# The last attention head's first three query blocks in the 64x64 form, and the pool of the feed-forward part's transposed rows opened after that head

## The chip, the cores and the metric

The kernel runs on one core of one Trainium2 chip. The metric is the device time of one execution in microseconds (us). Before the change three runs gave 1917.64, 1917.69 and 1917.80 us, so the median is 1917.69 us.

## The reference

`x` has 2048 rows of 640 numbers, there are 32 heads of width 192 with 2048 cached keys and values each, and everything is bfloat16.

```python
xn = layernorm(x)                              # no scale, no shift
q  = (xn @ wq) split into 32 heads of 192
p  = softmax(q @ k_cache^T * 192**-0.5)        # per head, 2048 x 2048
s  = concat_heads(p @ v_cache) @ wo            # 2048 x 640
h  = silu(xn @ w1) * (xn @ w3)                 # 2048 x 1536
g  = silu(h @ w2)                              # 2048 x 640
out = x + s * g
```

## The kernel before

**Tiling.** The 2048 queries are worked in four blocks of 512 (`qb` 0 to 3). In one block of one head the 2048 keys are taken in 8 pairs of 2 x 128 (`p` 0 to 7). For each pair `scores` (L545) makes a 128 x 1024 tile `st` in PSUM, two of which exist; `weights` (L564) sends it through ScalarE's exponential into `pT2` (bf16), and the values are multiplied with `pT2` a pair or two later. At `p == 1` of each block one chunk of other matmuls is slipped in by `extra` (L1006): the query projection of the next head (`project_chunk`, L366), or in the last head (`h` = 31) the first 128 columns of the feed-forward part that no head carries (`hidden_last`, L958, its results `gl`, `ul` and at last `hx`).

**Two forms.** `in_quads` (L157) is true for heads 1 to 30 and false for heads 0 and 31.

- In the 64x64 form (`values_quads`, L627) the values are the stationary operand: twelve matmuls 64x64x512 for a pair, four running at once in the quarters of the array. Scores and projection are cut in 64x64 pieces as well. The output stands transposed (width by query) in two PSUM banks. `evict_quads` (L658) copies one half of a bank with ScalarE (`oa`), adds the other with VectorE (`ot`), and SyncE's queue issues a DMA transpose into `ox`. The sums of the softmax's rows do not come from the matmul: `row_sums` (L672) adds the weight tiles on VectorE (`tree`, then `e`), a second DMA transpose brings `e` to `eT`, and `turned_sums` (L709) reduces `eT` to `rs`, takes reciprocals and writes the scaled rows of `ox` to the staging tile `ostage`: five VectorE instructions. It is put down to run `NPAIR + 3` = 11 steps after `e`.
- In the other form (`values`, L608) the weights are the stationary operand and a column of ones in the value tile gives the row sums; a pair takes sixteen matmuls 64x128x193, two at a time. `evict` (L588) adds the halves on VectorE (`osum`) and scales them into `ostage` directly.

When both heads of a group of two have filled an `ostage` tile, `staged` (L579) stores it to `o_scr` in DRAM.

**Order.** Instructions under `pin` keep the order in which the code is run on their engine. `later` (L669) puts work in a list with a due step, and `do_chores` (L730) runs what is due at the end of each step, one step being one pair. Each engine works through its own list in order, and so does SyncE's DMA queue: a DMA whose data are not ready holds up those behind it.

**Around the last head.** Sixteen groups of 64 columns of the feed-forward part, one for each pair of heads, are made by `swiglu_chunk` (L527) in the odd heads and stored to `hT_scr` when a pair of heads is done; in the last head two chunks each are made in blocks 0 and 1 (`chunks`, L997). At the start of its block 2 the pool of the transposes' and row sums' tiles is closed (`astack.close`) and the pool `hTp` for the feed-forward rows is opened in its room. After the head, `load_hT` reads `hT_scr` back to `hT`, and `ffn_hidden` (L932) makes the rest. Its first call is laid between the last parts of the head's values by `by_halves` (L338): ten matmuls (first half), then a VectorE copy of one column, `mark` (L353), that waits for them, meanwhile eight value matmuls, and then the second ten, whose first one waits for `mark`. The names `w1_sb`, `w2_sb` and `w3_sb` all appear as `w_sb` in the profile. `w2_sb` (1920 KB, L1082) is loaded by POOL's queue into the room of `xnS`, as soon as TensorE has read `xnS` for the last time, which is in `hidden_last` of block 3.

Of the kernel before, what the change touches and what calls it, by code (L numbers as in the profile page):

```python
# [30 lines left out]
def _kernel_impl(ctx, tc, A_x, A_k_cache, A_v_cache, A_wq, A_wo, B_w1, B_w3, B_w2, out):  # L31
    nc = tc.nc
    _, SQ, D = A_x.shape
    _, H, SK, dh = A_k_cache.shape
# [3 lines left out]
    FC = F // P  # L38
    NQT = SQ // P
    NQB = SQ // 512  # L40
    NKT = SK // P
    NPAIR = NKT // 2
# [8 lines left out]
    FCP = FPIG // P  # L51
# [24 lines left out]
    pin = tc.keep_in_program_order  # L76
# [5 lines left out]
    fstack = ExitStack()  # L82
# [73 lines left out]

    def in_quads(h):  # L157
        return 0 < h < H - 1

    def load_ahead(h, qb):  # L160
        if qb == 0:
# [11 lines left out]
    with ExitStack() as actx:  # L173
# [150 lines left out]
        acc = {}  # L324

        def start_head(h):
            L = loads.pop(h)
            heads[h] = dict(
                h=h, L=L, quads=in_quads(h),
                qA=qp.tile([P, SQ], BF16, tag="qA", name="qA"),  # L330
                qF=qfp.tile([P, SQ], BF16, tag="qF", name="qF"),
                qS=qp.tile([P, SQ], BF16, tag="qS", name="qS"),
                qD=qp.tile([DT, SQ], BF16, tag="qD", name="qD"),
                st=stt.tile([P, 5, NQB], F32, tag="st", name="st"),
            )
            pin(nc.vector.memset(heads[h]["st"][:], 0.0))
# [20 lines left out]
        def by_steps(halves, w, qs, quads):  # L357
            for s in range(2 * DC):
                for c in ROWS if quads else (slice(0, P),):
                    for t in range(2):  # L360
                        xs = xnT if s % 2 == t else xnS
                        pin(nc.tensor.matmul(halves[t][c, :], lhsT=w[ROWS[t], s, c], rhs=xs[ROWS[t], s // 2, qs],  # L362
                                             start=(s == 0), stop=(s == 2 * DC - 1)))
# [215 lines left out]
        def staged(h, qb):  # L579
            stages[h // HG, qb][1] -= 1  # L580
            if stages[h // HG, qb][1] == 0:
                g0 = h - h % HG
                keep = pin if in_quads(h) else (lambda x: x)
                acc["store"] = keep(nc.sync.dma_start(
                    out=o_scr[qb].rearrange("(t p) c -> p t c", p=P)[:, :, g0 * DH:(g0 + HG) * DH],
                    in_=stages.pop((h // HG, qb))[0][:, :, :]))
# [82 lines left out]
        def later(wait, f, *a):  # L669
            chores.append((clock[0] + wait, f, a))  # L670
# [4 lines left out]
        def row_sums(hd, qb, p, w):  # L675
            sm = hd["sums"]

            def fours():
                t = aq["tree"].tile([P, 2, 1024], BF16, tag="tree", name="tree")
                a, b = sm["w"]  # L680
                sm["w"] = []
                add(t[:], a[:], b[:])
                sm["t"].append(t)

            def join():
                a, b = sm["t"]
                add(a[:], a[:], b[:])
                sm["t"].pop()

            def fold():  # L690
                t = sm["t"][0]
                add(t[:, 0, :], t[:, 0, :], t[:, 1, :])

            def ends():
                t = sm["t"].pop()[:, 0, :]
                e = aq["two"].tile([P, 512], BF16, tag="e", name="e")
                add(e[:], t[:, 0:512], t[:, 512:1024])
                eT = aq["two"].tile([P, 4, P], BF16, tag="eT", name="eT")
                pin(nc.sync.dma_start_transpose(out=eT[:], in_=e[:]))
# [26 lines left out]
        clock = [0]  # L726
        chores = []
# [12 lines left out]
        heads = {}  # L740
        parts = []
# [11 lines left out]

        def step(hd, qb, p, extra=None):
            me = (hd["h"], qb)
            first = qb == 0 and p < 2
            st2 = scores(hd, qb, p, quads=before["quads"] if first else hd["quads"])
            old = [k for k, _ in parts if k != me]
            old_quads = bool(old) and heads_quads(old[0][0])
            if p == 1 and old_quads:  # L760
                while parts[0][0] != me:
                    next_part()
            pT2 = weights(st2, hd["nb"][qb], p)
            while late:
                late.pop(0)()
            parts.extend((values_quads if hd["quads"] else values)(hd, qb, p, pT2))
            if hd["quads"] and p % 2 == 1:
                row_sums(hd, qb, p, acc["w"])
            if p == 0:
                while sum(k != me for k, _ in parts) > (2 if old_quads else 1):  # L770
                    next_part()
            elif p == 1:
                while parts[0][0] != me:
                    next_part()
            else:
                while len(parts) > (4 + (p > 2) if hd["quads"] else 3):
# [8 lines left out]
        heads_quads = in_quads  # L785
        before = {"quads": False}

        start_head(0)
        L0, m0 = heads[0]["L"], heads[0]["st"][:, 0:3, 0]
# [124 lines left out]
        astack = ExitStack()  # L914
# [40 lines left out]

        last = {}

        def hidden_last(qb, quads):  # L958
            w, g, u = last["w"], last["g"], last["u"]
            qs = slice(qb * 512, (qb + 1) * 512)  # L960
            ps = ps_st.tile([P, 1024], F32, tag="st2", name="ps")
            by_steps((ps[:, 0:512], ps[:, 512:1024]), w, qs, quads)
            pin(nc.vector.tensor_copy(out=g[:, qs], in_=ps[:, 0:512]))
            pin(nc.vector.tensor_copy(out=u[:, qs], in_=ps[:, 512:1024]))

            def gate():
                t = fsb.tile([P, 512], BF16, tag="t", name="t")
                pin(nc.scalar.activation(out=t[:], in_=g[:, qs], func=ACT.Tanh, scale=0.5))

                def product():  # L970
                    a = fsb.tile([P, 512], BF16, tag="a", name="a")
                    pin(nc.vector.scalar_tensor_tensor(out=a[:], in0=t[:], scalar=1.0, in1=g[:, qs], op0=ALU.add, op1=ALU.mult))
                    pin(nc.vector.tensor_tensor(out=hx[:, qs], in0=a[:], in1=u[:, qs], op=ALU.mult))
                return product
            return gate

        for h in range(1, H):
# [16 lines left out]
                todo = [h + 1]  # L994
            else:
                lengths = todo = []
            chunks = [[0], [1], [2], [3]] if h + 1 < H else [[0, 1], [2, 3], [], []]  # L997
            gated = []
            for qb in range(NQB):
                post = []  # L1000
                if (h, qb) == (H - 1, 2):
                    while chores:
                        clock[0] += 1
                        do_chores(h, qb, 2)
                    astack.close()
                    acc["hTp"] = fstack.enter_context(tc.tile_pool(name="hTp", bufs=2, side="right"))  # L1006

                def extra():
                    if h % 2 == 1:
                        for c in chunks[qb]:  # L1010
                            gate = swiglu_chunk(h // 2, heads[h - 1]["qF"], hd["qF"], c)
                            gated.append(gate if hd["quads"] and h > 1 else gate())
                    quads = before["quads"] if qb == 0 else hd["quads"]
                    if h + 1 < H:
                        post.append(project_chunk(h + 1, qb, quads=quads, cast_low=nc.scalar.copy if hd["quads"] else None))
                    else:
                        post.append(hidden_last(qb, quads))

                for p in range(NPAIR):
                    step(hd, qb, p, extra if p == 1 else None)  # L1020
# [14 lines left out]
                        loads[3].update(load_keys(3))  # L1035
                    if (h, qb, p) == (1, 2, 7):
                        copy_keys(3, loads[3])
                    if h + 1 < H:
                        if p == 3 and gated:
                            if hd["quads"] and h > 1:  # L1040
                                later(1, lambda f=gated.pop(0): gated.append(f()))
                            later(3, lambda: gated.pop(0)())
                    else:
                        if p > 4 and gated:
                            gated.pop(0)()
                        if p == 3:
                            gated.append(post.pop()())
# [2 lines left out]
                f(*a)  # L1050
                assert 0, "late"
            heads.pop(h - 1, None)
            before["quads"] = hd["quads"]

        def load_hT(qb):
            for f0, f1 in ((0, FCP // 2), (FCP // 2, FCP)) if qb < NQB - 1 else ((0, FCP),):
# [351 lines left out]
```

## Time and profile before

| | |
|---|---|
| median of 3 runs | 1917.69 us |
| profiled execution | 1917.67 us |
| its span in the trace | 1916.1 us |
| DVE (VectorE) busy | 1438.6 us |
| ACT (ScalarE) busy | 1388.5 us |
| last head, about | 1577 to 1629 us of the span |
| feed-forward rest, about | 1629 to 1705 us |
| output projection | 1705 us to the end |

Times inside the trace count from the start of the span. In a row of a timeline the first number is the start, the second the duration; the bracket at the end tells how long the engine had been idle and what ended that. `PE` is TensorE, `PEld` its weight loads, `SPq` is SyncE's DMA queue, `POOLq` GpSimd's. In a DMA row "to landing" is the time from issue until the data have arrived.

### The profile page before, as it was taken

To read this page: it belongs to the slowest core of one execution; us is meant where nothing else is said; L and a number is where in the kernel's file an instruction comes from. 1 tells how busy PE (TensorE), PEld (TensorE's weight loads), DVE (VectorE), ACT (ScalarE), POOL (GpSimd) and SP (SyncE) were. 2 spreads that over 40 slices of the span, in tenths; PEclk is the share of its full clock that TensorE was granted. 3 is DMA by queue.
4 is the path that set the end of the run, shared out by engine and by line. 5 is a ranking of instruction groups with operands and counts; after the bars stand their busy time and mean duration, and the time that the engine had idled before them with its cause. 6 is when DMAs were issued, how large, how long until landed. Compare 5 with 4: busy or idle time off the path is not lost.

```text
span 1916.1 us, 69138 instructions
## 1 busy us (share of the span) xinstructions
PE 1910.5 (100%) x31063; PEld 1243.5 (65%) x31063; DVE 1438.6 (75%) x2570; ACT 1388.5 (72%) x1533; POOL 141.1 (7%) x223
## 2 busy tenths in 40 slices
PE   9999999999999999999999999999999999999999
PEld 5666666666666666666666666666666666454446
DVE  8688888888888888888888888888888886521111
ACT  7888888888888888888888888888888887210000
POOL 3300000000000000000000000000000000000000
PEclk9999999999999999999999999999999999999999
DMA  7855665656565647565756565656656634936763
GB/s 171 154 98 105 127 120 115 123 114 121 119 127 105 137 101 136 100 136 105 138 99 140 100 129 105 129 105 134 112 115 125 120 69 125 278 76 149 166 151 78
DMA packets 655979, 237.44 MB, mean 124 GB/s; under 512 B 583472, under 2 KB 647568, under 8 KB 655680
## 3 DMA queue, kind: packets, MB, share of 16 engines
q1 hardware_dynamic: 647216, 212.55, 56.1%
q0 software_dynamic: 3776, 15.40, 2.7%
q8 instruction: 243, 3.98, 0.9%
q10 hardware_dynamic: 4688, 5.05, 0.8%
q14 instruction: 56, 0.46, 0.1%
HBM read 54.26 MB, written 31.98 MB: 45 GB/s over the span
## 4 chain that ended last, share of the span: by engine, by line
PE 99%; POOL 0%; DMA 0%; ACT 0%; issue 0%; SPq 0%; DVE 0%; POOLq 0%
PE st L561 34%; PE obank L640 32%; PE ps L362 14%; PE ps_s L1152 8%; PE ps_s L1108 3%; PE obank L620 2%; PE ps_f L1172 2%; PE ps_gu L940 1%; PE ps_f L1188 1%; PE ps L347 0%; DMA KT<-in_A_k_cache_dram 0%; PE ps_gu L347 0%; ACT xnT L290 0%; SPq L115 0%; PE pst L289 0%
## 5 line engine op out<-in xcount | busy, mean ns | idle before, releaser
L569 ACT ACTIVATE pT<-st,nb 128x1024 bf16<-128x1024 f32 x1016 | 1125.4, 1113 | 182.4 <-PE st L561 148.6
L640 PE MATMUL obank<-pT,vt 64*64 64x512 bf16 x11520 | 811.3, 376 | 0.0
L640 PEld LDWEIGHTS <-vt 64*64 64x64 bf16 x11520 | 428.7, 107 | 210.6
L561 PE MATMUL st<-qS,KM 64*64 64x512 bf16 (+1 forms) x1983 | 417.5, 376 | 0.1
L561 PE MATMUL st<-qD,KT 64*64 64x512 bf16 (+1 forms) x1983 | 417.4, 376 | 0.0
L561 PE MATMUL st<-qA,KT 64*64 64x512 bf16 (+1 forms) x1983 | 417.4, 376 | 0.0
L561 PE MATMUL st<-qA,KM 64*64 64x512 bf16 (+1 forms) x1983 | 391.2, 376 | 0.0
L561 PE MATMUL st<-qS,KT 64*64 64x512 bf16 (+1 forms) x1983 | 391.0, 376 | 0.1
L561 PE MATMUL st<-qF,KT 64*64 64x512 bf16 (+1 forms) x1983 | 391.0, 376 | 0.0
L561 PEld LDWEIGHTS <-KT 64*64 64x64 bf16 (+1 forms) x7936 | 289.9, 107 | 138.8 <-issue 0.6
L673 DVE TENSOR_TENSOR tree<-pT,pT 128x2048 bf16<-128x2048 bf16 x240 | 291.8, 1216 | 3.9 <-ACT pT L569 3.4
L362 PE MATMUL ps<-xnT,wq 64*64 64x512 bf16 (+1 forms) x2430 | 292.0, 376 | 0.0
L362 PE MATMUL ps<-xnS,wq 64*64 64x512 bf16 (+1 forms) x2430 | 287.9, 376 | 0.0
L665 DVE TENSOR_TENSOR ot<-oa,obank 128x512 bf16<-128x512 f32 x240 | 154.2, 684 | 147.3 <-ACT oa L664 147.3
L362 PEld LDWEIGHTS <-wq 64*64 64x64 bf16 (+1 forms) x4860 | 176.8, 107 | 89.6
L673 DVE TENSOR_TENSOR tree<-tree 128x2048 bf16<-128x2048 bf16 x240 | 228.9, 954 | 4.1
L561 PEld LDWEIGHTS <-KM 64*64 64x64 bf16 (+1 forms) x3968 | 152.6, 106 | 59.1 <-issue 1.5
L1152 PE MATMUL ps_s<-oT,wo_sb 128*128 128x512 bf16 x720 | 155.7, 379 | 0.0
L664 ACT COPY oa<-obank 128x512 f32<-128x512 f32 x240 | 127.8, 588 | 0.0
L1152 PEld LDWEIGHTS <-wo_sb 128*128 128x128 bf16 x720 | 70.4, 98 | 84.9 <-issue 0.2
L385 ACT CAST qF<-ps 128x512 bf16<-128x512 f32 x127 | 74.5, 586 | 59.3 <-PE ps L362 59.3
L1142 DVE SCALAR_TENSOR_TENSOR tmp<-ps_s,gT 128x512 f32<-128x512 f32 x15 | 10.3, 687 | 136.0 <-PE ps_s L1152 136.0
(159 smaller groups left out, 1427.8 us busy)
## 6 DMA issues: line engine op xcount, KB each, us to landing
o_scr<-ostage SPq DMA_DIRECT2D x64, 384.0 KB, 4.4
vt<-in_A_v_cache_dram SPq DMA_DIRECT2D x62, 384.0 KB, 5.1
qS<-qA SPq DMA_DIRECT2D x240, 64.0 KB, 2.0
qD<-qF SPq DMA_DIRECT2D x120, 64.0 KB, 2.1
KM<-KT SPq DMA_DIRECT2D x60, 128.0 KB, 5.0
wo_sb<-in_A_wo_dram POOLq DMA_DIRECT2D x1, 7680.0 KB, 30.1
wq<-in_A_wq_dram SPq DMA_DIRECT2D x29, 160.0 KB, 3.7
hT_scr<-hblk SPq DMA_DIRECT2D x16, 256.0 KB, 3.2
```

What stands on the lines that cost most here:

```text
L362: pin(nc.tensor.matmul(halves[t][c, :], lhsT=w[ROWS[t], s, c], rhs=xs[ROWS[t], s // 2, qs], start=(s == 0), stop=(s == 2 * DC - 1)))
L385: pin(c(out=dst[:, qs], in_=src))
L561: pin(nc.tensor.matmul(st2[c, t * 512:(t + 1) * 512], lhsT=k[:, c], rhs=q[ROWS[t], qs], start=(s == 0), stop=(s == 2)))
L569: pin(nc.scalar.activation(out=pT2, in_=st2[:], func=ACT.Exp, scale=SCALE, bias=nb[:]))
L620: pin(nc.tensor.matmul(acc["o"][b][:, r, (j % 2) * 256:(j % 2) * 256 + DH + 1], lhsT=pT2[ROWS[r], t * 512 + j * P:t * 512 + (j + 1) * P], ...
L640: pin(nc.tensor.matmul(acc["o"][low][ROWS[c], r, :], lhsT=vt[ROWS[r], u, p, c0:c0 + DT], rhs=pT2[ROWS[r], u * 512:(u + 1) * 512], start=(p ...
L664: pin(nc.scalar.copy(out=oa[:], in_=bank[:, 0, :]))
L665: pin(nc.vector.tensor_tensor(out=ot[:, k * 512:(k + 1) * 512], in0=oa[:], in1=bank[:, 1, :], op=ALU.add))
L673: pin(nc.vector.tensor_tensor(out=out, in0=a, in1=b, op=ALU.add))
L1108: pin(nc.tensor.matmul(ps, lhsT=oT[:, k, :], rhs=wo_sb[:, k, c0:c1], start=(k == 0), stop=(k == OC - 1)))
L1152: pin(nc.tensor.matmul(ps_of[d], lhsT=wo_sb[:, k, d * P:(d + 1) * P], rhs=part(k // KQ)[:, k % KQ, :], start=(k == 0), stop=(k == OC - 1)))
L1172: pin(nc.tensor.matmul(ps[:, e * 512:(e + 1) * 512], lhsT=w2_sb[:, fc, d * P:(d + 1) * P], rhs=rhs[fc], start=(fc == 0), stop=(fc == FC - 1)))
```

## The change

The form is now asked for by block: `block_quads(h, qb)` is true for heads 1 to 30 and also for blocks 0, 1 and 2 of head 31. Block 3 of head 31 stays in the other form.

```diff
+    def block_quads(h, qb):
+        return in_quads(h - 1) if qb < 0 else in_quads(h) or (h == H - 1 and qb < NQB - 1)
...
-                later(NPAIR + 3, turned_sums, hd, qb, eT)
+                later(NPAIR + 3 if block_quads(hd["h"], qb + 1) else 4, turned_sums, hd, qb, eT)
...
         def step(hd, qb, p, extra=None):
             me = (hd["h"], qb)
-            first = qb == 0 and p < 2
-            st2 = scores(hd, qb, p, quads=before["quads"] if first else hd["quads"])
+            quads = block_quads(*me)
+            st2 = scores(hd, qb, p, quads=block_quads(hd["h"], qb - 1) if p < 2 else quads)
...
-            parts.extend((values_quads if hd["quads"] else values)(hd, qb, p, pT2))
-            if hd["quads"] and p % 2 == 1:
+            parts.extend((values_quads if quads else values)(hd, qb, p, pT2))
+            if quads and p % 2 == 1:
                 row_sums(hd, qb, p, acc["w"])
...
-        def hidden_last(qb, quads):
+        def hidden_last(qb, quads, now):
...
             by_steps((ps[:, 0:512], ps[:, 512:1024]), w, qs, quads)
+            if now:
+                pin(nc.scalar.copy(out=u[:, qs], in_=ps[:, 512:1024]))
             pin(nc.vector.tensor_copy(out=g[:, qs], in_=ps[:, 0:512]))
-            pin(nc.vector.tensor_copy(out=u[:, qs], in_=ps[:, 512:1024]))
+            if not now:
+                pin(nc.vector.tensor_copy(out=u[:, qs], in_=ps[:, 512:1024]))
...
-            chunks = [[0], [1], [2], [3]] if h + 1 < H else [[0, 1], [2, 3], [], []]
...
-                if (h, qb) == (H - 1, 2):
-                    while chores:
-                        clock[0] += 1
-                        do_chores(h, qb, 2)
-                    astack.close()
-                    acc["hTp"] = fstack.enter_context(tc.tile_pool(name="hTp", bufs=2, side="right"))
+                now = block_quads(h, qb)
...
-                    if h + 1 < H:
+                    if h + 1 < H or now:
                         if p == 3 and gated:
-                            if hd["quads"] and h > 1:
+                            if now and h > 1:
                                 later(1, lambda f=gated.pop(0): gated.append(f()))
                             later(3, lambda: gated.pop(0)())
+                        if p == 3 and h + 1 == H:
+                            later(3, lambda f=post.pop(): post.append(f()))
+                            later(4, lambda f=post: f.pop()())
...
-        assert FC - FCP == NQB
+        assert FC - FCP == NQB and not chores
+        astack.close()
+        acc["hTp"] = fstack.enter_context(tc.tile_pool(name="hTp", bufs=2, side="right"))
         load_hT(0)
```

In the last head one `swiglu_chunk` is now made in each of the four blocks, so the store to `hT_scr` follows block 3's. The row sums of block 2 are used 4 steps after their `e` and not 11.

On VectorE, at the end of the last head's block 3 before the change: `gl` and `ul` of block 3, then the scaling of block 2's second half, the gate's product (`a`, `hx`), and `mark`.

```order
L963 CAST gl_36485<-ps_38507 128x512
L964 CAST ul_36486<-ps_38507 128x512
L598 RECIPROCAL rl_all_73<-osum_38504 128x2
L599 TENSOR_TENSOR ostage_37897<-osum_38504,rl_all_73 128x2x192
L972 SCALAR_TENSOR_TENSOR a_38643<-t_38592,gl_36485 128x512
L973 TENSOR_TENSOR hx_1518<-a_38643,ul_36486 128x512
L353 COPY mark_38709<-eps_t_68 128x1
```

And there after the change, from the product of the last `swiglu_chunk` (`pa`, `hblk`) on. Ahead of these rows stand now, behind `gl` and `ul`, the end of block 2's row sums (two `tree` additions and `e`) and the five instructions of block 1's `turned_sums`. `eT_38694` and `ox_38602` belong to block 2.

```order
L543 SCALAR_TENSOR_TENSOR pa_38778<-pt_38610,qF_35281 64x512
L545 TENSOR_TENSOR hblk_37730<-pa_38778,qF_36488 64x512
L716 TENSOR_REDUCE rs_38807<-eT_38694 128x4
L718 RECIPROCAL rl_all_73<-rs_38807 128x4
L721 TENSOR_TENSOR ostage_37899<-ox_38602,rl_all_73 128x4x128
L724 TENSOR_TENSOR ox_38602<-ox_38602 128x4x64
L725 TENSOR_TENSOR ostage_37899<-ox_38602,rl_all_73 128x4x64
L975 SCALAR_TENSOR_TENSOR a_38814<-t_38720,gl_36485 128x512
L976 TENSOR_TENSOR hx_1518<-a_38814,ul_36486 128x512
L356 COPY mark_38862<-eps_t_68 128x1
```

Between `gl` and `mark` there now stand the row sums and both `turned_sums`, and the reduction that reads `eT_38694` and the scaling that reads `ox_38602` wait for DMA transposes of block 2.

On SyncE's DMA queue before the change, from the last head's last transpose on:

```order
L699 DMA_TRANSPOSE eT_37817<-e_37815 128x4x128
L584 DMA o_scr0_60<-ostage_37309 128x4x384
L1057 DMA hT_38695<-hT_scr_64 128x4x512
L1057 DMA hT_38735<-hT_scr_64 128x4x512
L544 DMA hT_scr_64<-hblk_37730 64x2048
```

And after the change, where six more transposes are in the queue, the last two of them here:

```order
L587 DMA o_scr0_60<-ostage_37309 128x4x384
L669 DMA_TRANSPOSE ox_38602<-ot_38601 128x8x128
L702 DMA_TRANSPOSE eT_38694<-e_38692 128x4x128
L587 DMA o_scr1_61<-ostage_37613 128x4x384
L547 DMA hT_scr_64<-hblk_37730 64x2048
L587 DMA o_scr2_62<-ostage_37899 128x4x384
L1055 DMA hT_38848<-hT_scr_64 128x4x512 x2
```

The store to `hT_scr` and all four loads of `hT` now stand behind block 2's transposes and behind the store of block 2's `ostage`.

More of the change, by code (lines that the diff above doesn't have):

```diff
@@ L755, in step @@
             me = (hd["h"], qb)
[L756 to L757 removed]
+            quads = block_quads(*me)
+            st2 = scores(hd, qb, p, quads=block_quads(hd["h"], qb - 1) if p < 2 else quads)
             old = [k for k, _ in parts if k != me]
[L759 removed]
+            old_quads = bool(old) and block_quads(*old[0])
             if p == 1 and old_quads:
@@ L1000, in _kernel_impl @@
                 post = []
[L1001 to L1006 removed]
+                now = block_quads(h, qb)
                 def extra():
                     if h % 2 == 1:
[L1010 to L1013, printed above, removed]
+                        gate = swiglu_chunk(h // 2, heads[h - 1]["qF"], hd["qF"], qb)
+                        gated.append(gate if now and h > 1 else gate())
+                    quads = block_quads(h, qb - 1)
                     if h + 1 < H:
[L1015 removed]
+                        post.append(project_chunk(h + 1, qb, quads=quads, cast_low=nc.scalar.copy if now else None))
                     else:
[L1017 removed]
+                        post.append(hidden_last(qb, quads, now))
                 for p in range(NPAIR):
```

9 lines of the change are left out of this document (3 added, 6 removed).

## The prediction

> **What bounds the kernel now.** I read the page first, then the chain of waits, then the timelines of the last head. The page's first group and the chain's shares by engine:
>
> ```profile
> PE 1910.5 (100%) x31063; PEld 1243.5 (65%) x31063; DVE 1438.6 (75%) x2570; ACT 1388.5 (72%) x1533; POOL 141.1 (7%) x223
> PE 99%; POOL 0%; DMA 0%; ACT 0%; issue 0%; SPq 0%; DVE 0%; POOLq 0%
> ```
>
> TensorE is never without work, and the chain that ends last is TensorE for 99% of the span. So a TensorE instruction saved is time saved, whatever another engine does extra is free, and a wait forced on TensorE is paid in full. Both signs must be looked for there. The chain's pieces "in order of time" give the length of a block, since the projection stands at `p == 1` of each: the gaps below are one block of head 30, then blocks 0, 1 and 2 of head 31.
>
> ```profile
> 1565.12 2.16 PE ps L362 x40
> ...
> 1577.64 2.16 PE ps L362 x40
> ...
> 1590.46 2.16 PE ps L362 x20
> ...
> 1603.14 2.16 PE ps L362 x20
> ...
> 1615.81 2.16 PE ps L362 x20
> ```
>
> Differences: 12.52 us in the 64x64 form, 12.82 where the form changes, then 12.68 and 12.67 in the other form.
>
> **Term 1, the form.** Blocks 0 to 2 took 12.82 + 12.68 + 12.67 = 38.17 us and will take 3 x 12.52 = 37.56. The change of form moves into block 3 and costs there 12.82 - 12.675 = 0.145 more than now. Sum: -0.61 + 0.145 = **-0.46 us**. That is all there is to gain: no other TensorE work goes.
>
> ScalarE and VectorE have to follow in the shorter blocks. VectorE gets `tree`, `e`, `ot` and `turned_sums` for `osum`, as in head 30, where this fits. ScalarE gets `oa`, `ul` and a second gate activation (`t`) a block. In head 29, which has one gate activation (`pt`) a block, the exponentials catch up:
>
> ```profile
> 1522.30 2.11 ACT L569 ACTIVATE pT<-st,nb 128x1024 bf16<-128x1024 f32 x2
> 1524.59 1.11 ACT L569 ACTIVATE pT<-st,nb 128x1024 bf16<-128x1024 f32 x1 [0.18 <-PE st L561]
> ```
>
> Two back to back take 2.11, so one costs 1.00 there against 1.29 of TensorE's time for a pair, and 0.18 us are idle. `t` now stands in that place and takes 0.52; the next exponential comes 0.34 late and the one after it is on time. `pt` delays one by about as much (0.29) and head 29's blocks are no longer for it, so I take nothing; if a delay of 0.34 showed in each of three blocks, it would be 1.0 us.
>
> **Term 2, the wait at the end of the head.** After block 3 the first feed-forward tile is made in two halves, and its second half waits for VectorE's `mark`:
>
> ```profile
> 1626.02 1.24 PE L347 MATMUL ps_gu<-xnT,w_sb 64*128 64x512 bf16 x10
> 1627.10 0.50 PE L620 MATMUL obank<-vt,pT 64*128 64x193 bf16 x8
> 1627.52 1.25 PE L347 MATMUL ps_gu<-xnT,w_sb 64*128 64x512 bf16 x10
> 1627.31 0.15 DVE L353 COPY mark<-eps_t 128x1 f32<-128x1 f32 x1 [4.18 <-PE ps_gu L347]
> ```
>
> Now VectorE is idle 4.18 us before `mark`, which ends at 1627.46; TensorE goes on 0.06 later. After the change the first half ends 0.46 earlier and the second could start at 1627.06. But by the order VectorE has, between block 3's `gl` and `mark`, the row sums of block 2, both `turned_sums`, and two products. I time them from block 0 of head 31, where block and form change as they now will in block 3, three blocks of 12.52 = 37.56 earlier:
>
> ```profile
> 1580.08 0.68 DVE L963 CAST gl<-ps 128x512 bf16<-128x512 f32 x1
> ...
> 1583.25 0.42 DVE L673 TENSOR_TENSOR e<-tree 128x512 bf16<-128x512 bf16 x1
> 1583.60 0.68 DVE L713 TENSOR_REDUCE rs<-eT 128x4 f32<-128x512 bf16 x1
> ...
> 1585.79 0.68 DVE L540 SCALAR_TENSOR_TENSOR pa<-pt,qF 64x512 bf16<-64x512 bf16 x1
> 1586.50 0.42 DVE L542 TENSOR_TENSOR hblk<-pa,qF 64x512 bf16<-64x512 bf16 x1
> ...
> 1587.90 0.68 DVE L972 SCALAR_TENSOR_TENSOR a<-t,gl 128x512 bf16<-128x512 bf16 x1
> 1588.61 0.42 DVE L973 TENSOR_TENSOR hx<-a,ul 128x512 bf16<-128x512 bf16 x1
> ```
>
> Shifted: `e` of block 2 ends at 1621.23; block 1's `turned_sums` (1583.60 to 1585.79 = 2.19) ends at 1623.35; `hblk` is done at 1624.4. From there block 2's `turned_sums` 2.19, `a` and `hx` 1.05, `mark` and 0.06: 3.46 us from the moment T at which its `rs` can start until TensorE's second half starts. If `eT` is there, T = 1624.41 and the half starts at 1627.87: 0.35 later than now. So **even undisturbed the wait (0.81) eats the 0.46**.
>
> T depends on when `eT` of block 2 lands. Its issue is at 1621.27, its `ox` goes out at 1617.75. Undisturbed, in block 0 of head 31 (views of SyncE's queue, and of the DMA issues and packets of 1580 to 1584 and of 1583.5 to 1587.5):
>
> ```profile
> 1580.19 1.23 SPq L666 DMA_TRANSPOSE ox<-ot  x1
> q1 hardware_dynamic: 1056, 0.26, 35.4%
> 1583.71 1.19 SPq L699 DMA_TRANSPOSE eT<-e  x1
> q1 hardware_dynamic: 544, 0.13, 31.5%
> ox<-ot SPq DMA_TRANSPOSE x1, 3.1
> eT<-e SPq DMA_TRANSPOSE x1, 3.2
> ```
>
> 1056 and 544 packets, 3.1 and 3.2 us; by the slices of the first view the 1056 move in 1.4 us and end 2.55 after issue, so 0.55 passes until the landing. 3.2 us for `eT` (block 2's would land at 1624.5). But POOL loads `w2_sb` just then, because it waits for the last read of `xnS`, in block 3's projection. Its issue, a store of SyncE's queue issued in the midst of it, their landings, and the packets of the two queues (q0 is POOL's) in 1620.5 to 1624 (one row) and in 1624 to 1626 (two):
>
> ```profile
> 1618.27 1.06 POOL L1082 DMA_DIRECT2D w_sb<-in_B_w_dram  x1 [53.39 <-PE ps L362]
> 1620.02 0.38 SPq L584 DMA_DIRECT2D o_scr<-ostage  x1
> w_sb<-in_B_w_dram POOLq DMA_DIRECT2D x1, 1920.0 KB, 8.9
> o_scr<-ostage SPq DMA_DIRECT2D x1, 384.0 KB, 7.9
> q0 software_dynamic: 217, 1.11, 89.7%
> q0 software_dynamic: 138, 0.70, 87.8%
> q1 hardware_dynamic: 122, 0.09, 13.9%
> ```
>
> In the first stretch SyncE's queue moved no packet at all, in the second 122 beside the load's 138, and the store landed at 1627.9, 0.7 after the load. So I expect the two transposes to be held until the load is through. The load moved data from about 1620.0 to 1626.4; the projection now ends 0.62 earlier (37.56 + 1579.80 against 1617.98), so to 1625.8. `ox` has some 0.45 us before it starts, 340 of its packets; during the load about 120 pass, as of that store; of 1600 some 1140 are left, at 1056 in 1.4 us another 1.5 us: 1627.3. With 0.6 from the last packet to the landing T = 1627.9, the second half starts at 1627.9 + 3.46 = 1631.36, a wait of 4.30. Everything behind follows TensorE and shifts alike.
>
> The bounds: T = 1624.4 (wait 0.81) and, if nothing passes beside the load and the landing tail is 1.4, T = 1629.1 (wait 5.5). Between stands the nearest case with a smaller load, 2 x 160 KB of `wl` at 1517.52:
>
> ```profile
> wl<-in_B_w_dram POOLq DMA_DIRECT2D x2, 160.0 KB, 4.1
> ox<-ot SPq DMA_TRANSPOSE x1, 5.5
> eT<-e SPq DMA_TRANSPOSE x1, 4.4
> ```
>
> There `ox` took 2.4 more than its usual 3.1 though the load was a sixth. I take the row with `w2_sb`, since it is the same load at the same place.
>
> [...]
>
> **Terms at nothing.** The loads of `hT` move behind `hblk`'s store and block 2's `o_scr` store:
>
> ```profile
> 1640.21 3.62 PE L1172 MATMUL ps_f<-hT,w_sb 128*128 128x512 bf16 x16
> hT<-hT_scr SPq DMA_DIRECT2D x2, 512.0 KB, 4.0
> ```
>
> `ostage` of block 2 is ready at T + 2.2 = 1630.1, the `hblk` store lands by about 1631, so the first `hT` lands at about 1636, and its reader is now at 1644: 8 us of cover. If that were gone, TensorE would wait for what is over. The other DMAs of the tail are released by TensorE's and VectorE's tail and shift with it. The pool opened later changes no instruction of TensorE.
>
> **Sum.** 1917.67 (this execution; the median is 1917.69) - 0.46 + 4.30 = **1921.5 us**.
>
> **Rivals.**
> (a) The transposes pass beside the load as if it were not there: T = 1624.4, 1917.67 - 0.46 + 0.81 = 1918.0, not slower in any way one could measure. For it: transposes move small packets in a queue of their own. Against it: the store that moved nothing. It decides if `eT` lands before about 1624.5.
> (b) They are held partly, as beside `wl`: `eT` 4.4 to 4.9 us, T = 1625.7 to 1626.2, 1919.3 to 1919.8.
> (c) Only the saving shows: `mark` isn't late, because T comes early and VectorE is ahead of block 0's pace: 1917.2. VectorE would have to gain 0.8 us; nothing shows that.
> (d) The wait also cools TensorE. At the start of the kernel, after 1.9 us of idleness, the same matmul is half as fast:
>
> ```profile
> 1.88 5.54 PE L224 MATMUL fill<-ones_w,ones_bf 128*128 128x512 bf16 x13 [1.88 <-DVE cols L189]
> 7.53 0.81 PE L224 MATMUL fill<-ones_w,ones_bf 128*128 128x512 bf16 x3
> ```
>
> 0.43 us each against 0.22 us later, though the profile's clock row stands at full there. If a gap of 4.3 us does the same, 3.4 to 5.5 us at half speed lose 1.7 to 2.8: 1923.2 to 1924.3. Against it: no gap in the trace lasts so long, so nothing shows when the speed falls. [...]
> (e) The change doesn't save on TensorE, since ScalarE's extra activation stalls it: +1.0 on the forecast, 1922.5.
>
> **Chances.** Forecast (held until the load is through, 1920.3 to 1922.8) 0.60, (a) 0.07, (b) 0.12, (c) 0.03, (d) 0.14, (e) 0.04. The range from 1918.0 to 1924.0 holds (a) to most of (d); the forecast's own range is 1920.3 to 1922.8. What can be told from no change is 0.2%, 3.84 us, so the line is at 1921.5, on the forecast itself: I give 0.37 of its 0.60 to the upper side (the bound above is as far as that below, but a landing tail is more easily longer than shorter), with (d) and (e) 0.55 slower, 0.43 within, and 0.02 faster, for which no row has the time.
>
> **What would show it.** Right: the projection chunks of head 31's blocks 0 to 2 12.52 apart; VectorE idle before the last `rs` until a DMA; `eT` of block 2 landing with or after `w2_sb`; `mark` starting near 1631; TensorE without work for about 4 us before the second half. Wrong: `eT` landing in 2.4 to 3.2 us; the second half at 1627.9 or earlier; a gap before `ps_f` that ends with a DMA of `hT`; blocks longer than 12.52 with idle TensorE at `st`; feed-forward matmuls at half pace behind the gap.

## The result and the profile after

| | before | after |
|---|---|---|
| time, median of the runs beside each other | 1917.73 us (6 runs, 1917.55 to 1917.84) | 1925.75 us (6 runs, 1924.92 to 1926.29) |
| ratio, 95% interval | | 1.0041 [1.003, 1.0052] |
| profiled execution, its span | 1917.67, 1916.1 | 1924.92, 1923.4 |
| mean granted clock | 1.0 | 0.998 or 0.999 in all six runs |

The change makes the kernel slower by 0.4%: 8.0 us in the medians, 7.25 in the two profiled executions, which the readings below account for. All times are us.

The chain of waits after, the pieces of the last two heads' projections and what follows them:

```profile
1564.94 2.16 PE ps L365 x40
...
1577.46 2.16 PE ps L365 x40
...
1589.98 2.16 PE ps L365 x40
...
1602.50 2.16 PE ps L365 x40
```

The gaps, one block of head 30 and then blocks 0 and 1 of head 31, are now all 12.52; before they were 12.52, 12.82 and 12.68. Block 2 takes 12.52 as well, by the first matmuls of its projection and of block 3's (1602.30 and 1614.82). The shorter form is there, and TensorE's rows from 1577 to 1625 show no stall beside it.

TensorE's timeline behind block 3, to be held against the rows of before in the prediction:

```profile
1625.38 1.24 PE L350 MATMUL ps_gu<-xnT,w_sb 64*128 64x512 bf16 x10
1626.46 0.50 PE L623 MATMUL obank<-vt,pT 64*128 64x193 bf16 x8
1632.18 2.32 PE L350 MATMUL ps_gu<-xnT,w_sb 64*128 64x512 bf16 x10 [5.23 <-DVE mark L356]
1634.29 1.50 PE L623 MATMUL obank<-vt,pT 64*128 64x193 bf16 x16
1635.73 11.26 PE L940 MATMUL ps_gu<-xnT,w_sb 128*128 128x512 bf16 x49
1646.83 3.62 PE L1172 MATMUL ps_f<-hT,w_sb 128*128 128x512 bf16 x15
```

Two things are to be seen. TensorE stands still for 5.23 before the second half of `ps_gu`. And that second half, ten matmuls that took 1.25 before, takes 2.32.

VectorE's timeline says what `mark` was behind:

```profile
1623.88 0.42 DVE L545 TENSOR_TENSOR hblk<-pa,qF 64x512 bf16<-64x512 bf16 x1
1628.71 0.69 DVE L716 TENSOR_REDUCE rs<-eT 128x4 f32<-128x512 bf16 x1 [4.42 <-DMA eT<-e]
...
1631.64 0.42 DVE L976 TENSOR_TENSOR hx<-a,ul 128x512 bf16<-128x512 bf16 x1
1631.98 0.15 DVE L356 COPY mark<-eps_t 128x1 f32<-128x1 f32 x1
```

VectorE itself idles 4.42, until the transpose `eT` of block 2 lands. From there to TensorE's second half pass 1632.18 - 1628.71 = 3.47.

The DMA issues of 1617 to 1630, with their size and the time to landing, then the packets of 1617 to 1620.5, of 1619 to 1621 and of 1621 to 1625 (q0 is POOL's queue with the load of `w_sb`, q1 is SyncE's with the transposes):

```profile
w_sb<-in_B_w_dram POOLq DMA_DIRECT2D x1, 1920.0 KB, 10.8
ox<-ot SPq DMA_TRANSPOSE x1, 7.9
eT<-e SPq DMA_TRANSPOSE x1, 7.6
```

```profile
q1 hardware_dynamic: 777, 0.20, 45.1%
```

```profile
q1 hardware_dynamic: 870, 0.22, 82.5%
q0 software_dynamic: 25, 0.13, 16.9%
```

```profile
q0 software_dynamic: 279, 1.43, 102.2%
q1 hardware_dynamic: 32, 0.00, 0.5%
```

Up to 1620.5 no packet of the load has passed. `ox` has 1056 packets, and 1024 of them are through by 1621. Then the load has the engines nearly to itself. The 32 packets of SyncE's queue in these 4 us are the last of `ox`, which lands at 1625.5; `eT` stands behind them. The first packet of the load comes at 1620.7, 3.2 behind its issue at 1617.48. In the ten profiles here in which no `ox` is under way at that time it comes 1.7 to 1.8 behind its issue (before: 1618.27 and 1620.00), in the four in which one is, 3.2 to 4.1 (after, e3, e4, e6).

The granted clock, in windows of 0.5 us (window, length, busy time of PE, PEld, DVE, ACT and POOL, then PEclk, DMA share and GB/s):

```profile
1629.00:1629.50 0.50, 0.00 (x0) 0.00 (x0) 0.47 (x2) 0.00 (x0) 0.00 (x0) 1.00 1.22 465
1629.50:1630.00 0.50, 0.00 (x0) 0.00 (x0) 0.47 (x2) 0.00 (x0) 0.00 (x0) 0.53 0.33 131
1632.50:1633.00 0.50, 0.50 (x4) 0.15 (x2) 0.00 (x0) 0.00 (x0) 0.00 (x0) 0.50 1.04 306
1636.00:1636.50 0.50, 0.37 (x2) 0.18 (x2) 0.50 (x2) 0.00 (x0) 0.12 (x1) 0.64 1.06 326
1636.50:1637.00 0.50, 0.50 (x3) 0.26 (x3) 0.47 (x2) 0.00 (x0) 0.50 (x2) 1.00 0.85 283
```

A window at 0.53 was at half clock for 94% of it, one at 0.64 for 72%. So the clock is halved from 1629.53 to 1636.36: it falls 2.6 after the last matmul ended and is back 4.2 after TensorE resumed.

The end of the program: VectorE's last instruction, and the last store, before and then after:

```profile
1913.26 0.29 DVE L1115 TENSOR_TENSOR res<-tmp,xt 128x128 bf16<-128x128 f32 x1
```

```profile
out_dram<-res ACTq DMA_DIRECT2D x1, 32.0 KB, 1.4
```

```profile
1919.88 0.29 DVE L1115 TENSOR_TENSOR res<-tmp,xt 128x128 bf16<-128x128 f32 x1
```

```profile
out_dram<-res ACTq DMA_DIRECT2D x1, 32.0 KB, 2.0
```

The account, before to after, in the profiled executions:

| piece | working | us |
|---|---|---|
| start of the kernel (not of the change: it differs from run to run) | projection in head 30's block 1 at 1539.91 against 1540.09 | -0.18 |
| shorter form | first half of `ps_gu` at 1625.38 against 1626.02, less the line above | -0.46 |
| wait for `mark` | first to second half 6.80 against 1.50 | +5.30 |
| half clock | second half to `ps_f` 14.65 against 12.69 | +1.96 |
| from `ps_f` to VectorE's last start | 273.05 against 273.05 | 0.00 |
| end | the rest of 7.25 | +0.63 |

### The profile page after: what moved, and what is told of

Read it like the earlier page. It is cut to its first block, busy times and chain, and to the rows that moved or that the text cites. A ratio compares the mean times of both kernels' runs of the same rounds, so it can differ in the third digit from the quotient of the medians.

```text
span 1923.4 us, 69363 instructions
## 1 busy us (share of the span) xinstructions
PE 1910.1 (99%) x31148; PEld 1243.6 (65%) x31171; DVE 1449.6 (75%) x2579; ACT 1392.4 (72%) x1542; POOL 141.1 (7%) x223
## 4 chain that ended last, share of the span: by engine, by line
PE 98%; DMA 1%; DVE 0%; issue 0%; ACT 0%; POOL 0%; SPq 0%; POOLq 0%
PE st L564 34%; PE obank L643 33%; PE ps L365 14%; PE ps_s L1152 8%; PE ps_s L1108 3%; PE ps_f L1172 2%; PE ps_gu L940 1%; PE obank L623 1%; PE ps_f L1188 1%; DMA eT<-e 0%; PE ps L350 0%; DMA KT<-in_A_k_cache_dram 0%; PE ps_gu L350 0%; DVE tree L676 0%; ACT pT L572 0%
## 5 line engine op out<-in xcount | busy, mean ns | idle before, releaser
L643 PE MATMUL obank<-pT,vt 64*64 64x512 bf16 x11808 | 831.6, 376 | 0.0
L643 PEld LDWEIGHTS <-vt 64*64 64x64 bf16 x11808 | 439.8, 107 | 216.1
L676 DVE TENSOR_TENSOR tree<-pT,pT 128x2048 bf16<-128x2048 bf16 x246 | 299.1, 1216 | 3.9 <-ACT pT L572 3.4
L668 DVE TENSOR_TENSOR ot<-oa,obank 128x512 bf16<-128x512 f32 x246 | 158.1, 684 | 151.3 <-ACT oa L667 151.3
L676 DVE TENSOR_TENSOR tree<-tree 128x2048 bf16<-128x2048 bf16 x246 | 234.6, 954 | 4.2
```

The lines of the kernel that those rows point to most:

```text
L643: pin(nc.tensor.matmul(acc["o"][low][ROWS[c], r, :], lhsT=vt[ROWS[r], u, p, c0:c0 + DT], rhs=pT2[ROWS[r], u * 512:(u + 1) * 512], start=(p ...
L668: pin(nc.vector.tensor_tensor(out=ot[:, k * 512:(k + 1) * 512], in0=oa[:], in1=bank[:, 1, :], op=ALU.add))
L676: pin(nc.vector.tensor_tensor(out=out, in0=a, in1=b, op=ALU.add))
```

## The experiments

Each ran beside the kernel before, whose median there was 1917.77 to 1917.83.

**e1, two blocks instead of three.** Blocks 0 and 1 of head 31 take the 64x64 form, block 2 doesn't, so that the `eT` of block 2 is not late.

```diff
-        return in_quads(h - 1) if qb < 0 else in_quads(h) or (h == H - 1 and qb < NQB - 1)
+        return in_quads(h - 1) if qb < 0 else in_quads(h) or (h == H - 1 and qb < NQB - 2)
```

> The 64x64 form in blocks 0 and 1 of the last head only; block 2 goes back to the other form, so its two transposes are gone, and the last pair of transposes is block 1's, issued about 12.5 us before w2_sb is loaded. Theory (TensorE loses by waiting for mark behind block 2's transposes, which the load of w2_sb holds up, and by the slow clock after it): no wait before the second half, clock full throughout, and two blocks' saving, 2 x 0.155 = 0.3 us: 1917.4 us. Rival 1 (the cost lies in the later opening of the pool and the later hT loads): still about 8 us slower than before. Rival 2 (the form itself saves nothing): 1917.7.

Measured: 1918.74 (1918.42 to 1919.05, 11 runs), ratio 1.0005 [0.9996, 1.0014]. TensorE does not wait for `mark` and the clock is 1.0 (0.999 in one run of eleven): wait and half clock both belong to the third block. But the two shorter blocks do not give their 0.30 + 0.16 - 0.145 = 0.31 either: the first half of `ps_gu` starts at 1626.11 in the chain against 1626.19, and 0.03 of that is the start. The chain leaves TensorE in block 2 and comes back to it in block 3:

```profile
1603.88 1.29 DVE ot L668 x2
...
1618.71 0.61 DVE ul L967
1619.36 0.82 PE st L564 x6
```

For 15 us it runs over VectorE, which has the row sums of two blocks one behind the other there, and the six `st` at its end take 0.82, where the next six take 0.65. That this is where the rest of the 0.31 went is read from the chain alone; no run tried it. The remaining 0.8 to before arises after VectorE's last row (see g1 and g2).

**e2, the code of the change with the form of before.** `block_quads` gives `in_quads(h)`, so that only the later opening of the pool and the code paths remain.

```diff
-        return in_quads(h - 1) if qb < 0 else in_quads(h) or (h == H - 1 and qb < NQB - 1)
+        return in_quads(h - 1) if qb < 0 else in_quads(h)
```

> Everything of the change but the form: blocks 0 to 2 in the form of before, one feed-forward chunk in each block of the last head, the pool opened behind the head, the store of hblk and the hT loads late. Theory: no term in the time, 1917.7 us within 0.3. Rival (late hT loads or the pool stall the feed-forward part): a gap at ps_f and up to 8 us more.

Measured: 1917.81 (1917.67 to 1918.41, 11 runs), ratio 1.0 [0.9991, 1.0009]; first half of `ps_gu` at 1626.03 against 1626.02. This part costs nothing.

**e3, an attempt to hold the load.** The load of `w2_sb` written to be issued after block 2's `rs`.

```diff
-    nc.gpsimd.dma_start(out=w2_sb[:], in_=B_w2.rearrange("(c p) d -> p c d", p=P))
+    with tc.issue_after(acc["rs"].ins):
+        nc.gpsimd.dma_start(out=w2_sb[:], in_=B_w2.rearrange("(c p) d -> p c d", p=P))
```

> As after, but POOL issues the load of w2_sb only when VectorE has read block 2's eT. Theory: ox and eT land in 3.1 to 3.2 us, T is 1624.4 in the frame of before, the wait shrinks from 5.2 to about 0.8 us and the clock stays full: 1918.0 us, and w2_sb lands at about 1634, before its first reader. Rival (the transposes are slow for a reason of their own, not for the load): eT still takes over 7 us and the time stays at 1925 or more.

Measured: 1925.58 (1924.97 to 1927.4, 5 runs), ratio 1.0042 [1.0028, 1.0055]. The edit set an order among instructions but no wait: the load went out at 1617.89, right behind the last projection, as without it. So nothing was held, and this is the changed kernel once more. It shows how far the two transfers vary: in its profile `eT` took 9.1 to land, `w_sb` 12.4, and TensorE waited 6.76.

**e4, `mark` by ScalarE.** The same ineffective hold, and `mark` copied by ScalarE, so that TensorE's second half no longer stands behind VectorE's row.

```diff
-                          nc.vector.tensor_copy, between)
+                          nc.scalar.copy, between)
```

> As the run with the load held, and mark is made by ScalarE, idle at that place, instead of VectorE. Theory: the remaining 0.8 us of wait goes too and only the form's saving is left: 1917.2 us, less than before. Rival (VectorE's late work is paid in the next wait, for the tiles ps_gu that it empties): 1917.5 to 1918.

Measured: 1923.3 (1922.22 to 1924.68, 8 runs), ratio 1.0027 [1.0017, 1.0038]. The second half starts at 1627.08 without a wait, and TensorE waits a little later instead, for a `ps_gu` tile that VectorE has to empty. Its VectorE and TensorE rows:

```profile
1630.21 0.69 DVE L716 TENSOR_REDUCE rs<-eT 128x4 f32<-128x512 bf16 x1 [5.74 <-DMA eT<-e]
```

```profile
1634.80 5.52 PE L940 MATMUL ps_gu<-xnT,w_sb 128*128 128x512 bf16 x17 [3.54 <-DVE a L947]
```

So `mark` is only where the lateness of VectorE is met first. Its cause is ahead of VectorE.

**f5, the load really held.** A data wait of the load on block 2's `rs`, so that the transposes have the DMA engines without it.

```diff
-    nc.gpsimd.dma_start(out=w2_sb[:], in_=B_w2.rearrange("(c p) d -> p c d", p=P))
+    load = nc.gpsimd.dma_start(out=w2_sb[:], in_=B_w2.rearrange("(c p) d -> p c d", p=P))
+    tc.add_manual_dep(load.ins, acc["rs"].ins.name, mybir.DependencyInfo(
+        mybir.DependencyClass.Sync, mybir.DependencyReason.DATA), reason="hold")
```

> The changed kernel, with the 1920 KB load of w_sb made to wait for the reduction rs of block 2, so that the transposes of ot and e of block 2 no longer share the DMA engines with it. Theory (the load holds the transposes up): eT lands in 2.5 to 3.3 us instead of 7.6, ox in about 3.1 instead of 7.9, rs starts near 1624.4 instead of 1628.7, TensorE's wait for mark falls from 5.23 to about 0.8, the granted clock stays at 1.0 throughout, and the time is 1917.9 to 1918.8. Rival (the transposes are late for a reason of their own, such as their queue or the store of hT): eT still takes over 6 us, the wait stays over 4 and the time at or above 1924. Third outcome: the load, now late, collides with the loads of hT, and TensorE waits ahead of the output blocks; then the wait for mark is gone and the time is still above 1919.5.

Measured: 1919.11 (1918.8 to 1921.78, 11 runs), ratio 1.0008 [0.9999, 1.0017]. The load is issued at 1625.88. The DMA issues of 1617 to 1640, VectorE and TensorE:

```profile
ox<-ot SPq DMA_TRANSPOSE x1, 3.9
eT<-e SPq DMA_TRANSPOSE x1, 2.4
```

```profile
1624.30 0.42 DVE L545 TENSOR_TENSOR hblk<-pa,qF 64x512 bf16<-64x512 bf16 x1
1624.64 0.67 DVE L716 TENSOR_REDUCE rs<-eT 128x4 f32<-128x512 bf16 x1
```

```profile
1628.10 1.25 PE L350 MATMUL ps_gu<-xnT,w_sb 64*128 64x512 bf16 x10 [0.72 <-DVE mark L356]
```

`eT` lands in 2.4 and not 7.6, `rs` follows `hblk` without a gap, the wait falls to 0.72 and the second half takes 1.25 again. The load now runs beside SyncE's stores and loads, which pass with it. The packets of 1631 to 1632:

```profile
q0 software_dynamic: 62, 0.32, 86.5%
q1 hardware_dynamic: 61, 0.05, 13.9%
```

That `eT` is on time as soon as the load is issued later shows the load as the cause of the late transposes. One run of the eleven, 1921.78, has a mean clock of 0.999; its gap is not known. No wait for `hT` appears. The time is 0.3 above what was expected, since the end of the program costs 1.0 here (last store 2.3).

**f6, the load held and `mark` by ScalarE.** Both edits above.

> As the run before, and mark is written by ScalarE instead of VectorE, so that TensorE's second half of the first ps_gu no longer stands behind rs, a and hx of block 2. Theory (the wait for mark is the transposes plus VectorE's row): no wait there at all, and some 0.8 less than the run before: 1917.2 to 1918.0. Rival (VectorE's lateness is only passed on to the next place that needs it, the ps_gu tile that VectorE empties): a wait of 0.5 to 1 us in the first ps_gu groups of L940 instead, and the same time as the run before.

Measured: 1918.38 (1918.07 to 1918.6, 11 runs), ratio 1.0003 [0.9994, 1.0012]: 0.73 less than f5. TensorE has no wait between 1617 and 1700. With the transposes in time, VectorE's own row behind `mark` was the last 0.72, and the tiles of L940 are emptied early enough. Yet it is not faster than before, since the end still costs 0.6.

**e6, TensorE kept busy in the gap.** The changed kernel, with 18 matmuls that nobody reads ahead of the wait.

```diff
+        def keep_warm():
+            parts.pop(0)[1]()
+            for _ in range(18):
+                pin(nc.tensor.matmul(warmer[:, 0:512], lhsT=ones_bf[:], rhs=xnT[:, 0, 0:512], start=True, stop=True))
...
-        rest = ffn_hidden(0, 1, ps_st.tile([P, 1024], F32, tag="st2", name="ps_gu"), parts.pop(0)[1])
+        rest = ffn_hidden(0, 1, ps_st.tile([P, 1024], F32, tag="st2", name="ps_gu"), keep_warm)
```

> The changed kernel, with 18 matmuls of 512 columns into a tile that nobody reads put between the two halves of the first ps_gu, ahead of the wait for mark (4 to 5 us of TensorE work at full clock). Theory (about 2 of the 8 us are a clock that halves because TensorE stood still for 5.2 us): mark comes no earlier, the second half starts at the same time (near 1632) but the granted clock stays at 1.0, and the time is 1.7 to 2.0 below the changed kernel's: 1923.5 to 1924.2. Rival (the half clock is not due to the standing still, or it delays nothing because the waits behind it take it up): 1925.4 to 1926.

Measured: 1923.73 (1923.06 to 1925.66, 6 runs), ratio 1.0032 [1.002, 1.0045], 2.0 below the changed kernel. TensorE's timeline:

```profile
1627.16 4.06 PE L1078 MATMUL warmer<-xnT,ones_bf 128*128 128x512 bf16 x17
1633.15 1.25 PE L350 MATMUL ps_gu<-xnT,w_sb 64*128 64x512 bf16 x10 [1.93 <-DVE mark L356]
1634.24 0.83 PE L623 MATMUL obank<-vt,pT 64*128 64x193 bf16 x16
1635.00 11.00 PE L940 MATMUL ps_gu<-xnT,w_sb 128*128 128x512 bf16 x49
1645.84 3.62 PE L1179 MATMUL ps_f<-hT,w_sb 128*128 128x512 bf16 x15
```

Here `mark` comes even 1.0 later (1633.15 against 1632.18), and still `ps_f` starts 1.0 earlier: from the second half to `ps_f` it takes 12.69, as before the change, and not 14.65. The half clock is a consequence of TensorE's standing still, and it costs 1.96. (In the medians part of the 2.0 is the end: this kernel's last store lands in 1.4.)

**e7 and e8, the wait alone.** The kernel before, with 11 and with 14 operations on VectorE ahead of `mark`; no transfer and no form is changed.

```diff
+        for _ in range(11):
+            junk = fsb.tile([P, 512], BF16, tag="u", name="junk")
+            pin(nc.vector.scalar_tensor_tensor(out=junk[:], in0=xnT[:, 0, 0:512], scalar=1.0, in1=xnT[:, 1, 0:512], op0=ALU.add, op1=ALU.mult))
```

> The kernel before, with 11 extra VectorE operations of 512 elements per partition queued ahead of mark, so that TensorE waits for mark as in the change, but for VectorE's work alone and with no transfer moved: a wait of about 2.5 us. Theory (a standing TensorE costs its wait, and keeps its clock if the gap stays below the 2.6 us after which it halved in the changed kernel): time above before by the wait as the waits show it, 1920.0 to 1920.6, clock 1.0 throughout. Rival (each such gap costs more than itself): over 1921.5.

> The run before with 14 instead of 11 extra VectorE operations: a wait of about 4.5 us at the same place. Theory (past some 2.6 us of standing still the clock halves for some 7 us, as in the changed kernel): a half clock in the trace between about 1629.5 and 1636.5, and the time above before by the wait plus 1.7 to 2.0: 1924.0 to 1924.4. Rival (the half clock needs the changed kernel's transfers or its other form): clock 1.0 throughout and the wait alone, 1922.1 to 1922.5.

Measured: e7 1920.92 (1919.82 to 1922.06, 10 runs), ratio 1.0015 [1.0006, 1.0025]; e8 1923.63 (1923.18 to 1923.69, 7 runs), ratio 1.003 [1.0019, 1.0041]. The median of e7 describes no run: its runs fall in two groups of five, 1919.82 to 1920.29 with a mean clock of 1.0 and 1921.55 to 1922.06 with 0.999. The profiled one is of the second group; the gaps of the others are not known. TensorE's waiting row and the clock of e7:

```profile
1630.11 1.83 PE L347 MATMUL ps_gu<-xnT,w_sb 64*128 64x512 bf16 x10 [2.27 <-DVE mark L353]
```

```profile
1630.00:1630.50 0.50, 0.39 (x4) 0.21 (x6) 0.05 (x1) 0.00 (x0) 0.00 (x0) 1.00 0.00 0
1630.50:1631.00 0.50, 0.50 (x7) 0.22 (x4) 0.00 (x0) 0.00 (x0) 0.00 (x0) 0.65 0.00 0
...
1634.00:1634.50 0.50, 0.50 (x4) 0.26 (x3) 0.47 (x2) 0.00 (x0) 0.50 (x2) 0.94 0.00 0
```

A gap of 2.27 costs 2.3 in half of the runs (1917.83 + 2.27 = 1920.1) and some 1.5 more in the other half. In the profiled one of these the clock falls at 1630.65, when TensorE is already working again, and is back at 1634.06: 3.4 later. In e8 the gap is 4.07, all seven runs have the half clock, it lasts from 1631.21 to 1634.62, again 3.4, and 1917.83 + 4.07 + 3.4 / 2 = 1923.6, as measured. The rival for e8, that the changed kernel's transfers or form are needed, falls; so does my bound of 2.6 in e7, under which a gap would keep its clock. In the changed kernel the half clock lasts 6.8, twice 3.4.

**f9, g1 and g2, the last 0.6.** f9 is the kernel before with 11 small copies more on ScalarE. g1 is f6 with the 13 filler matmuls at TensorE's start cut into 31 of 215 columns, 36 instructions more. g2 is the kernel before with them cut into 121 of 56 columns, 216 instructions more, which is as many as the change adds.

```diff
-        keep_busy(13)
+        keep_busy(31, 215)
```

> The kernel before, with 11 copies of one element per partition by ScalarE added in the output stage, where ScalarE has time to spare (some 0.2 us each). Theory (the 0.6 to 0.8 us at the very end of the changed kernel is one more fetch of instructions, 16 KB, for ScalarE's longer program, which lands between the last stores): TensorE's part ends within 0.1 of before, the last store takes 2.0 instead of 1.4, and the time is 1918.3 to 1918.6. Rival (the end belongs to the change itself, or to another engine's program): 1917.6 to 1917.9.

> The run with the load held and mark on ScalarE, and the 13 filler matmuls of 512 columns with which TensorE begins replaced by 31 of 215 columns (the same columns, 36 more instructions of TensorE). Theory (the 0.6 at the very end is a fetch of TensorE's instructions, 16 KB at a time, that falls between the last two stores; 36 more instructions bring it forward by 18 times 52.32 / 384 = 2.5 us): the fetch lies near 2 us ahead of VectorE's last instruction, the last store takes 1.4 again, 2.8 to 3.0 us from VectorE's last start to the end of the span instead of 3.46, and 1917.6 to 1917.9, some 0.6 below that run and level with before. Rival (the end has nothing to do with the length of TensorE's program): 1918.2 to 1918.6.

> The kernel before, with the 13 filler matmuls of 512 columns at TensorE's start replaced by 121 of 56 columns, so that TensorE's program is exactly as long as the changed kernel's (216 instructions more) and nothing else differs. The start may come some us later or earlier by this, and is left out of the reading. Theory (as in the run before): from VectorE's last start to the end of the span it takes 3.4 to 3.6 us as in the changed kernel, instead of 2.84, and the last store 2.0 instead of 1.4, with a fetch packet between the last two stores. Rival: 2.8 to 2.9, and 1.4.

Measured: f9 1917.79 (11 runs), ratio 1.0 [0.9991, 1.0009]: 11 more instructions of ScalarE do nothing. g1 1917.63 (1917.42 to 1917.85, 11 runs), ratio 0.9999 [0.999, 1.0008]: 0.75 below f6. g2 1919.18 (1918.73 to 1920.21, 11 runs), ratio 1.0007 [0.9998, 1.0016]; 0.69 of it is a later start (1540.78 against 1540.09). VectorE's last row and the last store of g1, then of g2:

```profile
1913.11 0.29 DVE L1117 TENSOR_TENSOR res<-tmp,xt 128x128 bf16<-128x128 f32 x1
```

```profile
out_dram<-res ACTq DMA_DIRECT2D x1, 32.0 KB, 1.4
```

```profile
1913.96 0.29 DVE L1115 TENSOR_TENSOR res<-tmp,xt 128x128 bf16<-128x128 f32 x1
```

```profile
out_dram<-res ACTq DMA_DIRECT2D x1, 32.0 KB, 2.2
```

g2's span ends at 1917.6, 3.64 behind its row, where before it is 2.84. The queue that the page lists as `instruction` (q8) moves one packet near the end in each of the fourteen kernels. In before, e2, e6 to e8, f9 and g1 it moves some 1.5 to 1.8 ahead of the start of VectorE's last row and the last store takes 1.4 or 1.5; in after, e1, e3, e4, f5, f6 and g2 it moves 0.2 to 0.3 behind that start, about when the last store goes out, and that store takes 2.0 to 2.4. The kernel before gets the late packet when nothing but the filler matmuls of TensorE's start is cut into more instructions, f6 loses it in the same way. So the place depends on TensorE's program. That the packet carries TensorE's own instructions, and that it is what holds the store, is argued from the two always going together; no row names the engine. Why it falls in one of two places stays open: e1, with 144 instructions more than before, has it where 216 more have it, so it does not simply move with their number.

## Why the prediction was wrong

Forecast 1921.5 with 1918.0 to 1924.0; it was 1925.75. The direction was right, slower by over 0.2%, and so was the mechanism of the wait; the half clock behind the wait and the end were left out of the sum. That was -0.46 + 4.30 = 3.84 against 7.25 in the profile. The 3.41 between them are 1.00 of wait, 1.96 of half clock and 0.63 at the end, less 0.18 of an earlier start.

- **What bounds the kernel: right.** What TensorE lost in waits and in clock came out in the time in full, and the 273.05 from `ps_f` to VectorE's last row did not change by 0.01. Only the end lies outside TensorE.
- **Term 1: right,** -0.46, with blocks of 12.52 and no stall behind ScalarE's extra activation. Rival (e) falls with it.
- **Term 2, the chain: right.** From `rs` to the second half 3.46 were forecast and 3.47 measured. The undisturbed case was timed at T = 1624.41 and a wait of 0.81; f5 has 1624.64, less its 0.24 later start 1624.40, and 0.72.
- **Term 2, the hold: right in kind, 1.0 too small.** `eT` was held until the load was nearly through, as forecast (32 packets of SyncE's queue against 279), not passed (rival a) nor held partly (b). The step that failed is the load's timing: I let it run as before but 0.62 earlier, from 1619.4 to 1625.8, with 340 packets of `ox` ahead of it. But it was `ox` that held the load first: 1024 of its packets had passed by 1621, the first of the load came at 1620.7, and it took 10.8 to land instead of 8.9. Fewer packets were left behind it than the 1140 of the sum, yet `eT` landed 1.0 later than forecast. From 1621 to 1625 SyncE's queue moved 32 packets against the load's 279, but what it had ready there beyond the 32 is not known. In f5 from 1631 to 1632 it moved 61 against 62. So the runs show that the queues hold each other up, and not by what rule.
- **The clock: the step that failed most.** Rival (d) had the mechanism and its price (1.7 to 2.8; measured 1.96), but stood at 0.14 and as an alternative to the forecast. It came in all six runs, and it adds to the wait. No row gave that chance; it was my estimate, and the only row on it (matmuls of 0.43 against 0.22 later, after 1.9 of idleness at the start of the kernel) spoke for more. Of the 3.4 to 5.5 at half speed behind the price, only the 5.5 stood on a row of before (13 matmuls in 5.54 at the start), the 3.4 on none; the runs showed 3.4 in e7 and e8, and 6.8 in the changed kernel. They also show that the fall is not tied to the gap's start, and that TensorE can be at work when it comes: in e7 it had stopped at 1627.85 and worked again from 1630.11, and the clock fell at 1630.65. With this wait the clock fell in five runs of ten, with e8's 4.07 in seven of seven. What sets the moment of the fall is not shown.
- **The end: missing.** The terms at nothing let the tail's DMAs "shift with it". The last store did, but the packet of the instruction queue that it meets did not. 0.63 in the profile, a term that the sum put at nothing.
- **The range.** Its upper end took the longest wait or the forecast's wait with the half clock, not the longest wait with the half clock: from my own bounds that would have been 1917.67 - 0.46 + 5.5 + 2.8 = 1925.5, still short of 1925.75. With the measured price it is 1924.7, and the end's 0.63 leads to 1925.3.

## What to carry to other kernels

A gap on TensorE is to be priced as its length plus the half clock that can come with it. In this kernel none came with 1.93 (e6's profiled run, a clock of 1.00 from 1626.5 to 1650), it came in five runs of ten with e7's wait (2.27 in the profiled one) and in all seven with 4.07: 3.4 us at half speed, 1.7 lost (e8), or twice that stretch, part of it within the gap, 1.96 lost (the changed kernel). A small transfer that an engine waits for should not be issued beside a large load on another queue: here the 128 KB of `eT` took 7.6 instead of 2.4. Holding the load, moving `mark` to ScalarE and keeping the late packet of the instruction queue clear of the last store gave back all of the loss (g1, 1917.63), but the 0.46 of the shorter form did not become a gain that these runs can tell from no change.

## What was not expected of the hardware

- A small transfer can hold a large one up, and then be held by it: beside `ox` the first packet of the load came 3.2 to 4.1 behind its issue (four profiles) and not 1.7 to 1.8 (ten), and from 1621 to 1625 the load moved 279 packets against 32 of the transposes' queue.
- With a gap of 2.27 (in the profiled run) the clock halves in half of the runs, with one of 4.07 in all; the half clock begins at a time that is not the gap's (2.6 after the last matmul in the changed kernel, 3.7 in e8, 2.8 in e7, with TensorE at work again).
- A packet of the instruction queue (q8, 16.4 KB each: 4.00 MB in 244 packets in the changed kernel) at the very end goes with 0.6 to 1.0 more for the last store: 2.0 to 2.4 where the packet comes 0.2 to 0.3 behind the start of VectorE's last row, 1.4 or 1.5 where it comes 1.5 to 1.8 ahead of it.
